# Attention and experts on one core: rank the experts three slots earlier, split the early weight pieces in halves, free the output scatters of one another, and run the 256-row group ahead of the 128-row one

## The chip, the cores and the metric

One core of one Trainium2 chip runs the whole program. The metric is the device time of one execution in microseconds (us), the median of several runs. Lower is better. PE is the matmul engine (TensorE), DVE VectorE, ACT ScalarE, POOL GpSimd, and SP SyncE, which here only issues DMAs.

## The reference

Attention over 8 batches of 8 heads, 576 positions of 64 numbers, with a mask by blocks of 64; its output, 4608 rows of 512 numbers, goes through a layer of eight experts, of which each row uses the one with the highest logit.

```python
scores = scale * np.matmul(q, k.transpose(0, 1, 3, 2))
scores = np.where(mask, scores, -1000000000.0)      # block_i >= block_j
attn = np.exp(scores - np.max(scores, axis=-1, keepdims=True))
attn = attn / (np.sum(attn, axis=-1, keepdims=True) + 1e-09)
x = np.matmul(attn, v).transpose(0, 2, 1, 3).reshape(B * S, H * D)
logits = x @ w_gate + modality_bias[modality_id]
e_idx = np.argmax(logits, axis=1)
gate_w = probs[np.arange(N), e_idx]
for e in range(E):
    mask = e_idx == e
    h = np.maximum(x[mask] @ w1[e], 0.0)
    out[mask] = gate_w[mask, None] * (h @ w2[e])
```

## The kernel before

The program has two halves. The first is attention in 32 **slots**, one for each pair of heads, and one more slot that drains (`LAST`). A slot runs the pieces of two pairs, interleaved by the table `ORDER`: of pair `slot` the scores (`S0`, `S1`, ... on PE), the row maxima (`M`, DVE), the exponentials (`E`, ACT), the transposes (`T`) and their copies (`C`); of pair `slot - 1` the product with the values (`V`), its way back to rows (`B`, `Z0`, `Z1`). Two pieces run ahead. `L` loads q and k of pair `slot + 2` (tile `raw`, a DMA on SP's queue), and `Q` scales q of pair `slot + 1` on POOL (`scale`, line 193, four instructions). The scores of the next slot can't start before that scaling is done. Engines take their instructions in the order in which the code writes them.

After every four slots a batch is complete. Its rows are stored to the tensor `xrows` in HBM, and `routing` finds each row's expert and its place in that expert's list. The places are written to `idlist` in HBM by five indirect scatters on POOL for each batch (line 401). `choose` ranks the experts after three batches: the largest is "a", the next "b", and a third one, "c", gets what is chosen later.

While attention still runs, the experts' work is begun at the points that `EARLY_STEPS` names. `chosen` and `stage` read the rank into a register and load pieces of expert a's weights to one of two `staging` tiles. `prep` splits a piece on POOL into a high part (a cast, line 596) and a low part (a subtraction, line 597), four of each for a piece. `ids` loads the head of expert a's list, and `fetch` gathers rows by an indirect DMA on POOL (line 698).

The second half is the experts in **groups** of rows, one after another: a 256-row group and a 512-row group of the early ("lead") list, three 512-row groups of a, four of b, then a 128-row group that ends b's list, then a 256-row group of c. For each group:

- `gather` (line 698) brings the rows by indirect DMAs on POOL, four for each 128 rows, into the tile `xg[1]`, which is part of `xr`;
- `turn_rows` (lines 717 to 721) turns them in four steps (two for 256 rows): a transpose on DVE into a `room` of two buffers, a cast to the high part on ACT, and a subtraction for the low part on DVE;
- `up` (line 730) multiplies with the first weights, eight blocks of 12 matmuls, and takes each block out by ACT and DVE (lines 733, 734); the 128-row group has `up_few` and `turn_few` instead;
- `down` (line 770) multiplies with the second weights, scales by the gate on ACT (line 774) into one of four tiles `yos`, and scatters 128 rows to the output by an indirect DMA on POOL (line 775).

For group n the code writes first the gathers of group n + 1, then the `up`s of n, `turn_rows` of n + 1, and the second part of `down` of n with its scatters. The first gather of a list also calls `spread` (lines 681 to 690), which on POOL makes row numbers, ids and gates out of the list. All output scatters write one tensor, so by the framework's rule each waits for the landing of the one before. `declare_no_dep` takes that wait away; the scatters to `idlist` use it already (line 403).

Of the kernel before, what the change touches and what calls it, by code (L numbers as in the profile page):

```python
# [16 lines left out]
ALU = mybir.AluOpType  # L17
# [29 lines left out]
WIDE = 4  # L47
# [28 lines left out]
)  # L76

EARLY_STEPS = {
    (20, "S0"): ("chosen", "stage", "stage"), (21, "S0"): ("ids",), (21, "T0"): ("prep",),
    **{(slot, "T0"): ("stage", "prep") for slot in range(22, 29)},  # L80
    **{(slot, "S0"): ("fetch",) for slot in (23, 24, 25, 26, 27, 29, 31)},
    (30, "S0"): ("fetch", "stage"), (30, "T0"): ("fetch",) * 2, (31, "T0"): ("fetch",) * 2,
}
LAST = (
    ("+turn0", 0), ("V", 1), ("O", 1), ("D", 1), ("+up0", 0), ("+fetch3", 0), ("B", 1), ("Z0", 1), ("Z1", 1), ("+steps1", 0), ("+up1", 0), ("+fetch3", 0),
# [470 lines left out]
class Experts:  # L556
    def __init__(self, ctx, tc, cst, scratch, btmp, edges, xrows, idlist, idf, w1, w2, out, sel, run, base8, pick, dot, banks, ys, placing, staging, extra, xrb, xg0, steps_left):
        self.__dict__.update(locals())
        self.nc = tc.nc
        self.turn, self.hturn = 0, 0  # L560
        self.er, self.w = {}, {}
        self.staged = []
        self.todo = [(k, name, c) for name in "abc" for k in range(2) for c in range(4)]
        self.sturn, self.sbank = 0, 0
        flat = xrb[0].rearrange("p s q d -> p (s q d)")
        self.spare = xrb[1].rearrange("p s q d -> p (s q d)")
        self.turned = 0
        self.xg = [t.rearrange("p (c w) -> p c w", w=PIECE) for t in (xg0, flat[:, 0:2048])]
        self.yos = [t[:, 512 * i : 512 * i + 512] for t in (scratch, xg0) for i in range(2)]
        self.pieces = xrows.rearrange("n (i w) -> (n i) w", w=PIECE)  # L570

        def cut(i, a, n=1024):
            return extra[:, i : i + n].rearrange("p (a f) -> p a f", a=a)

        self.w["a", 1] = [[cut(1024 * (4 * x + c), 2) for c in range(4)] for x in range(2)]
        self.xth = cut(1024 * 8, 4, 2048)
        self.xtl = self.xth[:, :, 256:512]
        self.hidden = extra[:, 1024 * 10 : 1024 * 14]
        self.w["a", 0] = [cut(1024 * 14 + 4096 * x, 4, 4096) for x in range(2)]
        self.parts = []  # L580
# [5 lines left out]
    def early(self, what):  # L586
        if what == "stage":
            self.stage()
        elif what == "chosen":
            assert not self.steps_left("c")  # L590
        elif what == "prep":
            st, k, name, c = self.staged[0]
            flat = [t.rearrange("p a f -> p (a f)") if len(t.shape) > 2 else t for t in (st, *self.target(k, name, c))]
            for i in range(4):
                s, h, l = (t[:, 256 * i : 256 * i + 256] for t in flat)
                self.nc.gpsimd.tensor_copy(h, s)
                self.nc.gpsimd.tensor_tensor(l, s, h, ALU.subtract)
            self.staged.pop(0)
        elif what == "ids":
            ids = self.load_ids(self.sel["ra"], 0, LEAD, "lead", self.scratch[:, 512:1024])  # L600
            self.plan = [(ids, 0, "a", EARLY * S), (ids, 2, "a", EARLY * S, WIDE)]
        elif what[0:5] == "fetch":
            for _ in range(int(what[5:] or 1)):
                self.fetch_next()
        elif what[0:4] == "turn":
            self.turn_rows(self.parts[int(what[4])])
        elif what[0:2] == "up":
            for m in range(2):
                self.up(self.parts[0], 2 * int(what[2]) + m)
        elif what == "place":  # L610
            if self.placing:
                g, c = self.placing.pop(0)
                g(c)
        elif what == "flush":
            self.flush()
# [93 lines left out]
    def turn_rows(self, s):  # L709
        nc, n = self.nc, 4 * s.parts  # L710
        room = self.spare if self.turned else self.scratch
        self.turned += 1
        step = 1 if s.parts == WIDE else 2
        for k in range(0, 4, step):
            at = 512 * (k // step % 2)
            x = room[:, at : at + 32 * n * step].rearrange("p (k c t) -> p k c t", k=step, t=32)
# [1 line left out]
            xv = x.rearrange("p k c t -> p k (c t)")  # L718
            h, l = (t[:, k : k + step, 0 : 32 * n] for t in (self.xth, self.xtl))
            nc.scalar.copy(h, xv)  # L720
            nc.vector.tensor_tensor(l, xv, h, ALU.subtract)

    def up(self, s, m):
        nc, n = self.nc, 128 * s.parts
# [37 lines left out]
    def down(self, s, i, ms=range(8)):  # L762
# [7 lines left out]
            nc.tensor.matmul(y, s.hs[m][x][:, ts], self.part(w, 1, m // 2)[:, m % 2, :], start=first, stop=last)  # L770
        if ms[-1] != 7:
            return
        yo = self.yos[i]
        nc.scalar.mul(yo, y, s.list.gate[:, s.t + i : s.t + i + 1])
        nc.gpsimd.indirect_dma_start(self.out, bass.IndirectOffsetOnAxis(ap=s.list.ids[:, s.t + i : s.t + i + 1], axis=0), yo, None, bounds_check=N - 1, oob_is_err=False)  # L775

    def next_segment(self, name):
        dve, start = self.nc.vector, self.sel["start"]
# [17 lines left out]
    def lists(self):  # L796
# [10 lines left out]
        self.more = self.trips(left)  # L807
        self.plan += [(idsa, WIDE * t, "a", N, WIDE) for t in range(3)]
        self.plan += [(idsb, WIDE * t, "b", N, WIDE) for t in range(4)]
        self.plan += [(idsb, 4 * WIDE, "b", N, 1), (idsc, 0, "a")]  # L810

    def run_all(self, steps):
        tc, ctx, plan = self.tc, self.ctx, self.plan
# [13 lines left out]
        for n in range(1, len(plan)):  # L827
# [6 lines left out]
            else:  # L834
                for m in range(8):
                    self.up(s, m)
                    if m == 3:
                        for _ in range(2):
                            if self.staged:
                                self.convert()  # L840
                        if s.parts == WIDE:
                            for i in range(WIDE):
                                self.down(s, i, range(4))
            if nxt is not None:
                self.turn_rows(nxt)
            for i in range(s.parts):
# [81 lines left out]
```

## Time and profile before

| what | value |
|---|---|
| three runs, median (lowest to highest) | 733.03 us (731.99 to 733.95) |
| the profiled execution, its own time | 734.32 us |
| its span, first to last instruction | 732.4 us |
| PE busy | 702.7 us (96%) |
| DVE, ACT, POOL busy | 381.2, 334.6, 343.2 us |
| mean granted TensorE clock | 0.985 of full speed |

Busy times are shares of the whole span. A matmul's end is modelled, so a busy PE may still run slower than it could. What a stretch loses is therefore read from its length beside that of a like stretch, and from the idle times in it. The clock column says which share of full speed was granted: 1.00 is 2.4 GHz, and a mean between 0.5 and 1.00 is a stretch that was partly at 1.2 GHz.

### The profile page before, as it was taken

Reading aid. Unit: us, or ns where it says so; the run is one execution under the profiler, and the core shown is the slowest. Engines: PE = TensorE matmul, PEld = TensorE weight load, DVE = VectorE, ACT = ScalarE, POOL = GpSimd, SP = SyncE. Lnnn points to the kernel's source line nnn. Section 1 sums busy time; section 2 is a strip of 40 time slices with the busy share of each in tenths; the row PEclk is TensorE's granted clock in tenths of the full one; section 3 lists DMA queues with packets and bytes.
Section 4 is the critical chain, followed back from the end, with each engine's and each line's share of the span. In section 5 each row is a group of like instructions: output and inputs, shape, how many; then the busy total and the mean of one; then the engine's idle time right before and its main releaser. Section 6 shows DMA issues by size and latency. Waiting matters only on the chain. (4 is left out here: it accounts for less than half of the span.)

```text
span 732.4 us, 17917 instructions
## 1 busy us (share of the span) xinstructions
PE 702.7 (96%) x6880; PEld 578.8 (79%) x6880; DVE 381.2 (52%) x1069; ACT 334.6 (46%) x983; POOL 343.2 (47%) x454
## 2 busy tenths in 40 slices
PE   8999999999999899999999999999999999999594
PEld 5888888788878787878888888886888888888483
DVE  5888898898989798642422323213242331321130
ACT  5888877778777777221321313213132241312020
POOL 2223343252589996567356172561725437131501
PEclk9999999999999999999999999999999999999978
DMA  6376445446667573414032130311413123010100
GB/s 211 121 236 207 137 153 151 138 136 193 182 184 206 167 220 93 100 43 104 26 108 64 44 110 24 118 50 43 111 33 123 35 70 99 34 43 28 48 15 20
DMA packets 38472, 77.41 MB, mean 106 GB/s; under 512 B 8574, under 2 KB 20746, under 8 KB 38384
## 3 DMA queue, kind: packets, MB, share of 16 engines
q1 hardware_dynamic: 29264, 57.02, 25.8%
q0 software_dynamic: 9120, 19.22, 8.5%
q8 instruction: 55, 0.90, 0.5%
q14 instruction: 33, 0.27, 0.1%
HBM read 54.84 MB, written 21.95 MB: 105 GB/s over the span
## 5 line engine op out<-in xcount | busy, mean ns | idle before, releaser
L231 ACT ACTIVATE pm<-bank,nm 128x512 f32<-128x512 f32 (+3 forms) x320 | 155.5, 501 | 64.9 <-DVE nm L218 64.1
L734 DVE SCALAR_TENSOR_TENSOR extra<-bank,extra 128x512 fp32r<-128x512 f32 (+1 forms) x80 | 50.9, 637 | 213.7 <-ACT extra L733 213.6
L733 ACT ACTIVATE extra<-bank 128x512 fp32r<-128x512 f32 (+1 forms) x80 | 44.4, 555 | 214.4 <-PE bank L730 214.4
L218 DVE TENSOR_REDUCE nm<-bank 128x1 f32<-128x512 f32 (+3 forms) x320 | 120.6, 445 | 7.7 <-PE bank L211 7.6
L730 PE MATMUL bank<-extra 128*128 128x512 f32 (+1 forms) x416 | 105.9, 356 | 9.7 <-ACT extra L720 9.6
L193 POOL TENSOR_SCALAR q<-raw 128x144 f32<-128x144 f32 x124 | 68.1, 583 | 67.8 <-DMA raw<-qk 45.5
L211 PE MATMUL bank<-raw,q 64*64 64x512 f32 (+7 forms) x1280 | 91.1, 416 | 4.0 <-POOL q L193 3.3
L238 PE MATMUL bank<-cf,pm 128*128 128x128 f32 (+1 forms) x736 | 90.2, 277 | 2.1 <-ACT pm L231 2.1
L730 PEld LDWEIGHTS bank<-extra 128*128 128x128 f32 x416 | 71.7, 195 | 21.4 <-ACT extra L720 11.1
L238 PEld LDWEIGHTS bank<-cf,pm 128*128 128x128 f32 (+1 forms) x736 | 78.4, 140 | 10.9 <-ACT pm L231 7.0
L211 PEld LDWEIGHTS bank<-raw,q 64*64 64x64 f32 x1280 | 56.4, 136 | 34.2 <-issue 22.1
L698 POOL DMA_INDIRECT xr<-xrows,row_b x68 | 70.4, 1035 | 21.0 <-issue 19.5
L401 POOL DMA_INDIRECT idlist<-idt,pi x40 | 40.8, 1020 | 74.5 <-DVE pi L400 40.8
L257 PE MATMUL b<-pt,v 64*64 64x64 f32 (+3 forms) x896 | 75.4, 267 | 0.2
L257 PE MATMUL o<-pt,v 64*64 64x64 f32 (+3 forms) x896 | 70.6, 262 | 0.8 <-DVE gl L297 0.8
L243 DVE COPY pt<-bank 128x512 f32<-128x512 f32 (+1 forms) x96 | 59.0, 642 | 17.3 <-PE bank L238 11.3
L231 ACT ACTIVATION_READ_ACCUMULATOR pm<-bank,nm 128x1 f32 x320 | 65.2, 204 | 0.0
L730 PE MATMUL bank<-xtl,extra 128*128 128x512 f32 (+1 forms) x160 | 60.5, 378 | 0.0
L720 ACT CAST extra<-xr 128x512 fp32r<-128x512 f32 (+1 forms) x36 | 21.9, 609 | 84.2 <-DVE xr L717 84.2
L698 POOL DMA_INDIRECT xr<-xrows,row_a x48 | 50.8, 1058 | 15.2 <-issue 14.6
L770 PE MATMUL bank<-extra 128*128 128x512 f32 x240 | 56.0, 389 | 0.0
L257 PEld LDWEIGHTS b<-pt,v 128*64 128x64 f32 (+1 forms) x896 | 53.3, 136 | 3.0 <-DVE pos L380 0.2
(182 smaller groups left out, 1172.5 us busy)
## 6 DMA issues: line engine op xcount, KB each, us to landing
raw<-qk SPq DMA_DIRECT2D x31, 576.0 KB, 4.0
v<-vr SPq DMA_DIRECT2D x32, 384.0 KB, 3.8
staging<-w SPq DMA_DIRECT2D x48, 128.0 KB, 3.5
staging<-w SPq DMA_DIRECT2D x12, 512.0 KB, 3.8
xrows<-xr SPq DMA_DIRECT2D x16, 256.0 KB, 4.4
xrows<-xr SPq DMA_DIRECT2D x32, 128.0 KB, 2.6
idlist<-btmp SPq DMA_DIRECT2D x8, 304.0 KB, 3.8
xr<-xrows,row_b POOLq DMA_INDIRECT x68, 2.6
```

Of the source, the lines that this page charges most:

```text
L193: pool.tensor_scalar(d.q[:, i : i + 144], d.raw[:, i : i + 144], SCALE, None, ALU.mult)
L211: pe.matmul(place(s, a, b)[64 * t : 64 * t + 64], d.q[hs, D * s : D * s + D], d.k[hs, a:b], start=True, stop=True)
L218: dve.tensor_reduce(d.nm[:, i : i + 1], place(s, a, b), AX.X, ALU.max, negate=True)
L231: act.activation(d.pm[:, o : o + b - a], place(s, a, b), AF.Exp, bias=d.nm[:, s : s + 1], scale=1.0, accum_out=total)
L238: pe.transpose(banks[g][0:m, 128 * i : 128 * i + 128], d.pm[:, o : o + m], idf)
L243: dve.tensor_copy(dst, src) if g in ON_DVE else act.copy(dst, src)
L257: pe.matmul(o.rearrange("p (n c) -> p n c", c=64), d.v[rows, h, block, :], x, start=start, stop=stop)
L698: self.nc.gpsimd.indirect_dma_start(s.xg[:, i, :], None, self.pieces[0 : 4 * s.nrows, :], bass.IndirectOffsetOnAxis(ap=row, axis=0), bound ...
L730: nc.tensor.matmul(hp, w[:, kc, ms], x[:, kc, 0:n], start=i == 0, stop=i == len(mm) - 1)
L733: nc.scalar.activation(hh, hp, AF.Relu)
L734: nc.vector.scalar_tensor_tensor(hl, hp, 0.0, hh, ALU.max, ALU.subtract)
L770: nc.tensor.matmul(y, s.hs[m][x][:, ts], self.part(w, 1, m // 2)[:, m % 2, :], start=first, stop=last)
```

## The change

1. `EARLY_STEPS`: the ranking is read and two weight pieces are staged in slot 17 in place of 20; the list's head is loaded in slot 20 in place of 21. A `prep` now does half a piece (two casts and two subtractions), and the 16 halves stand in slots 18 to 30 (two in 19, 21 and 22, else one) where eight whole pieces stood in slots 21 to 28. The next piece is staged right behind a piece's second half. The first gathers move by a slot or less.
2. `turn_rows`: a step's subtraction is written behind the next step's transpose.
3. `down`: a 256-row group writes its results to `yos` 2 and 3. Scatters of the lists a, b and c are declared free of one another.
4. `lists` and `run_all`: the 256-row group of c runs ahead of the 128-row group of b, and the lists of b and c are spread in groups 2 and 3, ahead of their first gathers.

```diff
+HALVES = {18: 1, 19: 2, 20: 1, 21: 2, 22: 2, **{slot: 1 for slot in range(23, 31)}}
 EARLY_STEPS = {
-    (20, "S0"): ("chosen", "stage", "stage"), (21, "S0"): ("ids",), (21, "T0"): ("prep",),
-    **{(slot, "T0"): ("stage", "prep") for slot in range(22, 29)},
-    **{(slot, "S0"): ("fetch",) for slot in (23, 24, 25, 26, 27, 29, 31)},
-    (30, "S0"): ("fetch", "stage"), (30, "T0"): ("fetch",) * 2, (31, "T0"): ("fetch",) * 2,
+    (17, "S0"): ("chosen", "stage", "stage"), (20, "S0"): ("ids",),
+    **{(slot, "T0"): ("prep",) * n for slot, n in HALVES.items()},
+    **{(slot, "S0"): ("fetch",) for slot in range(23, 32)},
+    (30, "V"): ("fetch",), (31, "V"): ("fetch",), (31, "T0"): ("fetch",),
 }
...
-            for i in range(4):
+            for i in range(2 * self.half, 2 * self.half + 2):
                 s, h, l = (t[:, 256 * i : 256 * i + 256] for t in flat)
                 self.nc.gpsimd.tensor_copy(h, s)
                 self.nc.gpsimd.tensor_tensor(l, s, h, ALU.subtract)
-            self.staged.pop(0)
+            self.half = 1 - self.half
+            if not self.half:
+                self.staged.pop(0)
+                self.stage()
...
-        step = 1 if s.parts == WIDE else 2
+        step, lows = 1 if s.parts == WIDE else 2, []
...
             nc.scalar.copy(h, xv)
-            nc.vector.tensor_tensor(l, xv, h, ALU.subtract)
+            lows.append((l, xv, h))
+            if len(lows) > 1:
+                nc.vector.tensor_tensor(*lows.pop(0), ALU.subtract)
+        nc.vector.tensor_tensor(*lows.pop(0), ALU.subtract)
...
-        yo = self.yos[i]
+        yo = self.yos[i + 2 if s.parts == 2 else i]
...
+        if s.list.name in "abc":
+            for other in self.outs:
+                self.tc.declare_no_dep(last.ins, other.ins, reason="each token stands once in these lists")
+            self.outs.append(last)
...
-        self.plan += [(idsb, 4 * WIDE, "b", N, 1), (idsc, 0, "a")]
+        self.plan += [(idsb, 4 * WIDE, "b", N, 1)]
+        self.plan.insert(-1, (idsc, 0, "a"))
...
+            if n in (2, 3):
+                self.spread(self.plan[5 if n == 2 else 9][0])
             if nxt is not None:
                 self.turn_rows(nxt)
```

How the instructions stand is shown at three places. First, POOL's queue between the scaling of pair 26 and that of pair 27, before: two scatters of places (`idlist`), one whole weight piece, a gather, and the scaling (`q`), on which the scores of slot 27 wait.

```order
L401 DMA idlist<-idt,pi_3844 38912x16
L596 CAST extra<-staging_80 128x256
L597 TENSOR_TENSOR extra<-staging_80,extra 128x256
L596 CAST extra<-staging_80 128x256
L597 TENSOR_TENSOR extra<-staging_80,extra 128x256
L596 CAST extra<-staging_80 128x256
L597 TENSOR_TENSOR extra<-staging_80,extra 128x256
L596 CAST extra<-staging_80 128x256
L597 TENSOR_TENSOR extra<-staging_80,extra 128x256
L401 DMA idlist<-idt,pi_3845 38912x16
L698 DMA xg_82<-xrows,row_lead 128x128
L193 TENSOR_SCALAR q_105<-raw_103 128x144 x4
```

The same place after the change:

```order
L402 DMA idlist<-idt,pi_3858 38912x16
L597 CAST extra<-staging_81 128x256
L598 TENSOR_TENSOR extra<-staging_81,extra 128x256
L597 CAST extra<-staging_81 128x256
L598 TENSOR_TENSOR extra<-staging_81,extra 128x256
L402 DMA idlist<-idt,pi_3859 38912x16
L702 DMA xg_82<-xrows,row_lead 128x128
L194 TENSOR_SCALAR q_105<-raw_103 128x144 x4
```

Half the piece has gone from this place; it stands in an earlier slot.

Second, POOL's queue at the end of the program, before, from the gathers of the 128-row group (`row_b`, four of them) on: `out` is the output, `ids_b` and `ids_c` the lists that the scatters go by, `row_c` and `both_c` what `spread` makes.

```order
L698 DMA xr_83<-xrows,row_b 128x128 x4
L775 DMA out<-scratch,ids_b 4608x512 x2
L775 DMA out<-xg_82,ids_b 4608x512 x2
L687 TENSOR_SCALAR row_c<-xr_84 32x8 x4
L689 COPY both_c<-xr_84 32x4 x4
L690 CAST ids_c<-both_c 128x2
L698 DMA xr_83<-xrows,row_c 128x128 x8
L775 DMA out<-scratch,ids_b 4608x512
L775 DMA out<-scratch,ids_c 4608x512 x2
```

And after:

```order
L702 DMA xr_83<-xrows,row_c 128x128 x8
L782 DMA out<-scratch,ids_b 4608x512 x2
L782 DMA out<-xg_82,ids_b 4608x512 x2
L702 DMA xr_83<-xrows,row_b 128x128 x4
L782 DMA out<-xg_82,ids_c 4608x512 x2
L782 DMA out<-scratch,ids_b 4608x512
```

The eight gathers of c have moved ahead of the four scatters of the last 512-row group of b, and the spreading of c's list has left this place. The four gathers of the 128-row group now stand behind those scatters.

Third, DVE's queue where the 512-row group of the early list is turned, before (`xtl` is the low part) and after:

```order
L717 STREAM_TRANSPOSE xr_84<-xr_83 128x512
L721 TENSOR_TENSOR xtl<-xr_84,extra 128x512
L717 STREAM_TRANSPOSE xr_84<-xr_83 128x512
L721 TENSOR_TENSOR xtl<-xr_84,extra 128x512
L717 STREAM_TRANSPOSE xr_84<-xr_83 128x512
L721 TENSOR_TENSOR xtl<-xr_84,extra 128x512
L717 STREAM_TRANSPOSE xr_84<-xr_83 128x512
L721 TENSOR_TENSOR xtl<-xr_84,extra 128x512
```

The queue after the change, at the same group:

```order
L721 STREAM_TRANSPOSE xr_84<-xr_83 128x512 x2
L727 TENSOR_TENSOR xtl<-xr_84,extra 128x512
L721 STREAM_TRANSPOSE xr_84<-xr_83 128x512
L727 TENSOR_TENSOR xtl<-xr_84,extra 128x512
L721 STREAM_TRANSPOSE xr_84<-xr_83 128x512
L727 TENSOR_TENSOR xtl<-xr_84,extra 128x512
L728 TENSOR_TENSOR xtl<-xr_84,extra 128x512
```

Each subtraction stands one transpose later.

## Rows read from the trace of the kernel before

**Rows 1.** Waits of PE: who for whom, us in total, times, longest.

```profile
PE bank L730 <- ACT extra L720: 11.1, 5, 8.6
PE bank L211 <- POOL q L193: 3.3, 2, 1.8
```

**Rows 2.** Stretches, one attention slot each (19, 21 to 27): length, engines busy, clock, DMA.

```profile
core 0: us, PE busy (x) PEld busy (x) DVE busy (x) ACT busy (x) POOL busy (x), PEclk, DMA share, GB/s
171.90:180.62 8.72, 8.72 (x172) 7.40 (x166) 7.80 (x26) 7.60 (x27) 3.63 (x8) 1.00 0.47 136
189.17:197.91 8.74, 8.74 (x172) 7.45 (x167) 8.03 (x24) 7.45 (x27) 5.65 (x10) 1.00 0.50 150
197.91:206.72 8.81, 8.81 (x170) 7.10 (x164) 8.30 (x30) 6.61 (x26) 8.11 (x14) 1.00 0.94 239
206.72:217.22 10.50, 9.00 (x173) 7.53 (x163) 9.05 (x30) 7.97 (x27) 9.07 (x21) 1.00 0.51 150
217.22:225.76 8.54, 8.54 (x153) 7.15 (x157) 7.17 (x23) 6.51 (x25) 7.94 (x15) 1.00 0.66 208
225.76:234.71 8.95, 8.95 (x174) 7.57 (x165) 7.77 (x24) 7.49 (x27) 8.17 (x13) 1.00 0.60 190
234.71:245.42 10.71, 8.90 (x158) 7.26 (x156) 9.59 (x35) 7.34 (x27) 9.69 (x15) 1.00 0.91 278
245.42:256.11 10.69, 10.56 (x157) 8.39 (x158) 6.84 (x21) 7.25 (x25) 9.73 (x16) 0.84 0.24 70
```

**Rows 3.** Timeline of POOL: start, us, instruction, idle time before it and its releaser.

```profile
194.77 1.03 POOL L401 DMA_INDIRECT idlist<-idt,pi  x1 [2.89 <-DVE pi L400]
...
235.93 0.41 POOL L596 CAST extra<-staging 128x256 fp32r<-128x256 f32 x1
...
240.76 1.02 POOL L401 DMA_INDIRECT idlist<-idt,pi  x1 [0.15 <-DVE pi L400]
242.09 1.04 POOL L698 DMA_INDIRECT xg<-xrows,row_lead  x1 [0.30 <-issue]
243.16 2.20 POOL L193 TENSOR_SCALAR q<-raw 128x144 f32<-128x144 f32 x4
```

**Rows 4.** Waits of SP's queue for POOL's weight splits: total, times, longest.

```profile
SPq L659 <- POOL extra L597: 3.8, 2, 2.6
```

**Rows 5.** Timeline of DVE at the starts of `turn_rows`: lead's 512 rows, b's first, c.

```profile
316.99 0.71 DVE L717 STREAM_TRANSPOSE xr<-xr 128x512 f32<-128x512 f32 x1 [5.59 <-DMA xr<-xrows,row_lead]
318.44 0.69 DVE L721 TENSOR_TENSOR xtl<-xr,extra 128x512 fp32r<-128x512 f32 x1 [0.74 <-ACT extra L720]
...
494.06 0.71 DVE L717 STREAM_TRANSPOSE xr<-xr 128x512 f32<-128x512 f32 x1 [6.36 <-DMA xr<-xrows,row_b]
...
695.26 0.71 DVE L717 STREAM_TRANSPOSE xr<-xr 128x512 f32<-128x512 f32 x1 [11.45 <-DMA xr<-xrows,row_c]
```

**Rows 6.** Stretches of the experts' half, with the columns of rows 2.

```profile
320.77:333.77 13.00, 12.00 (x50) 8.77 (x48) 7.49 (x24) 4.20 (x7) 7.06 (x14) 1.00 0.19 63
410.00:420.88 10.88, 10.88 (x50) 9.01 (x49) 2.08 (x3) 2.61 (x5) 2.76 (x3) 1.00 0.19 73
497.05:512.16 15.11, 13.57 (x49) 9.86 (x48) 5.39 (x8) 5.62 (x10) 2.97 (x3) 0.89 0.14 52
682.20:696.67 14.47, 5.88 (x27) 4.34 (x25) 1.97 (x4) 1.20 (x2) 8.39 (x10) 0.87 0.09 24
696.67:711.73 15.06, 15.01 (x96) 14.27 (x97) 4.96 (x10) 3.89 (x9) 1.01 (x1) 0.78 0.05 18
711.73:722.80 11.07, 11.07 (x50) 8.83 (x48) 0.42 (x1) 1.07 (x2) 0.99 (x1) 1.00 0.04 15
722.80:732.40 9.60, 0.00 (x1) 0.00 (x0) 0.00 (x0) 0.69 (x1) 0.97 (x1) 0.73 0.05 20
```

**Rows 7.** Timeline of POOL: scatters to the lists, an output scatter, the spreading of c.

```profile
318.27 0.97 POOL L401 DMA_INDIRECT idlist<-idt,pi  x1 [0.31 <-issue]
...
672.43 1.00 POOL L775 DMA_INDIRECT out<-scratch,ids_b  x1 [2.52 <-DMA out<-scratch,ids_b]
...
680.47 0.97 POOL L687 TENSOR_SCALAR row_c<-xr 32x8 int32<-32x8 f32 x4
```

More of the change, by code (lines that the diff above doesn't have):

```diff
@@ L561, in __init__ @@
         self.er, self.w = {}, {}
-        self.staged = []
+        self.staged, self.half, self.outs = [], 0, []
         self.todo = [(k, name, c) for name in "abc" for k in range(2) for c in range(4)]
@@ L772, in down @@
             return
-        yo = self.yos[i]
+        yo = self.yos[i + 2 if s.parts == 2 else i]
         nc.scalar.mul(yo, y, s.list.gate[:, s.t + i : s.t + i + 1])
-        nc.gpsimd.indirect_dma_start(self.out, bass.IndirectOffsetOnAxis(ap=s.list.ids[:, s.t + i : s.t + i + 1], axis=0), yo, None, bounds_check=N - 1, oob_is_err=False)
+        last = nc.gpsimd.indirect_dma_start(self.out, bass.IndirectOffsetOnAxis(ap=s.list.ids[:, s.t + i : s.t + i + 1], axis=0), yo, None, bounds_check=N - 1, oob_is_err=False)
+        if s.list.name in "abc":
+            for other in self.outs:
+                self.tc.declare_no_dep(last.ins, other.ins, reason="each token stands once in these lists")
+            self.outs.append(last)
     def next_segment(self, name):
```

## The prediction

> **What bounds the kernel now.** PE does, nearly everywhere; what can be won is the time in which it stands still or runs slowly behind a stand-still. I read the waits of PE first [rows 1]. Two releasers matter: the cast in `turn_rows` (11.1 us in five waits, one of them 8.6) and the scaling of q on POOL (3.3 us in two). Idle time alone says too little, so each place is measured as a stretch, from one landmark on PE to the next, against a like stretch without trouble.
>
> In the attention half the landmarks are the first score matmuls of the slots [rows 2]. Undisturbed slots take 8.72, 8.74 and 8.81 us (19, 21, 22); the length goes round with the slot's place in its batch, so slots 23 and 27 are held against 19, 25 against 21, and 26 against 22. Then slot 23 loses 10.50 - 8.72 = 1.8, slot 25 0.2, slot 26 1.9 and slot 27 2.0 us. The reader is to see the POOL column in those rows: 9.07, 9.69 and 9.73 us busy in slots of 10.5 to 10.7. Slot 27 has another cause than slot 26: PE is busy for 10.56 of 10.69 us, but at a mean clock of 0.84. It pays for the pause at the end of slot 26 by running partly at 1.2 GHz.
>
> In the experts' half four blocks of `up` take 10.88 us when nothing waits [rows 6]. Where lead's 512-row group begins, the same four took 13.00; where b's first group begins, 15.11. Ahead of c's group 14.47 us pass in which only one `down` has work, 11.07/2 = 5.5 us by the two `down`s of c. Then c's `up`s take 15.06 us at a clock of 0.78. DVE's timeline tells why [rows 5]: at b's first group and at c the first transpose waited for the gathered rows, 6.36 and 11.45 us. At lead's group it waited too, and there the steps themselves then run one after another: 1.45 us from a transpose to its subtraction, of which 0.74 is waiting for the cast.
>
> **The change part by part.** *Halved pieces.* On POOL a whole piece takes 240.76 - 0.15 - 235.93 = 4.7 us, a scatter 1.0 and a gap, the gather 1.04 + 0.30, the scaling 2.2 [rows 3]. With two scatters a slot's list is thus about 10.6 us long, and slot 26, which has exactly this list, is 10.71 long. Half a piece leaves 8.3 us, under the 8.7 to 8.8 of PE. Slots 23 to 30 have half a piece each, so POOL catches up by 2.3 us in slot 23 already, and the scalings for slots 25 to 28 come in time. Gain: 0.2 + 1.9 + 2.0 = 4.1 us, the clock's part in it. Bounds: nothing, if something else on POOL keeps the scalings late, and 4.1.
>
> Slot 23 keeps its loss. Slots 21 and 22 have whole pieces still, and slot 23 begins with the spreading of the early list: from the scatter at 194.77, which waits for DVE in any case, to the scaling for slot 24 POOL's queue reads the same before and after. So 1.8 us stay. What follows such a pause is not fixed: behind slot 23 (1.5 us of pause) the clock row shows 1.00 and a slot of 8.54 us; behind slot 26 (1.8 us) it shows 0.84 and 2.0 us lost [rows 2]. I go by the row of slot 23: no drop. The Trainium skill ("TensorE: Matmul & The Clock Gate", section "What's actually happening") says that the activity monitor is free-running and does not restart with the kernel, so by it the same pause may lower the clock in one program and not in another. By that rule the surviving pause could cost 2.0 us more, as in slot 27; it is a rival below.
>
> *Ranking in slot 17, the list's head in slot 20.* The eight staging DMAs leave SP's queue at slot 20 and stand at slot 17, ahead of a `raw` load. DVE writes the rank in slots 14 to 16, so nothing waits for it. POOL has room for the first halves: it is busy for only 3.63 of 8.72 us in slot 19. Cost: nothing; without that cover, a scaling late by as much as the load is.
>
> *Staging behind the second half.* This adds a wait on SP: the DMA into a staging tile waits for POOL's subtraction of the same slot, and the loads of v and `raw` are queued behind it. Such waits exist before too, 3.8 us in two, the longest 2.6 [rows 4], and they held no score matmul. A `raw` load is issued two slots ahead of its scores and scaled one slot ahead, which leaves about a slot of slack. Cost: nothing, at most one slot's worth of lateness for each of the eight pieces.
>
> *`turn_rows` pipelined.* The transpose of the next step now fills the 0.74 us gap. From the rows' durations (0.71, 0.74, 0.69) four steps come to about 5.5 us in place of 8.2. At lead's 512-row group the rows arrive when they did, and the last low part is ready some 2.7 us sooner; PE lost 13.00 - 10.88 = 2.1 us there and loses nothing then. In the first turn of 256 rows, within slot 32, one of two such gaps goes: 0 to 0.7, taken as 0.4, since PE has other work beside it. Elsewhere the turn is hidden behind `down`, and gains nothing.
>
> *Scatters independent, lists spread early.* An output scatter waits 2.52 us for the one ahead to land [rows 7]; three such waits for each 512-row group go, 7.6 us by which the gathers behind them start earlier. The spreading of b's list leaves the path too. At b's first group the rows are thus there 7.6 us or more earlier, and PE lost 15.11 - 10.88 = 4.2 there. All of it comes back, the clock's part (0.89) with it. Whether the declaration takes effect, no output scatter shows; the bounds are 0 and 2.52 us each. I take 2.52, because scatters to the lists, which are declared so already, follow each other at 0.31 us of idle time. In the other groups nothing waits on PE, and nothing is gained.
>
> *c ahead of the 128-row group.* c's eight gathers came behind the four scatters of b's last group and the spreading at 680.47 [rows 7], when only the 128-row group covered them. Now they stand ahead of those four scatters, a whole 512-row group earlier. So the pause of 14.47 - 5.5 = 8.9 us goes, and so does the low clock behind it: 15.06 x (1 - 0.78) = 3.3 us. The four gathers of the 128-row group now come behind the scatters: 4 x 1.34 = 5.4 us and a landing, while PE has all of c's work, 15.06 - 3.3 + 11.07 = 22.8 us. They are in time. The new place of the results (`yos` 2 and 3) keeps c's scatters off the buffers that the 128-row group writes; no engine waits for that. The tail, 9.60 us from the last matmul to the end [rows 6], hangs on one gate multiplication and one scatter as before, and stays.
>
> **The sum.** 4.1 + 0.4 + 2.1 + 4.2 + 8.9 + 3.3 = 23.0 us. The profiled execution took 734.32 us (span 732.4 and 1.9 around it), which gives 711.3. It lies 1.3 us above the runs' median of 733.03, so the forecast for a median is **710.0 us**.
>
> **The rivals.**
> - *The clock drops behind slot 23.* For it: slot 27. Against it: slot 24 in this trace. 710.0 + 2.0 = 712.0 us. Chance 0.10.
> - *POOL stays late in slots 25 to 27*, because the halves moved into slots 18 to 22 leave a backlog there, or because DVE's scatter indices come late. For it: slots 21 and 22 keep whole pieces. Against it: 2.3 us are freed in every slot from 23 to 28. The 4.1 us stay away: 714.1 us. Chance 0.10.
> - *The 128-row group starves in c's place.* For it: its gathers stand behind four scatters. Against it: 22.8 us of cover for some 9 us. If half of c's old pause came back, 4.5 us: 714.5 us. Chance 0.06.
> - *Scatters still wait for one another.* Then 7.6 us a group remain on POOL, but c's gathers are moved all the same, and b's first group has the early spreading and the shorter turn: 1 to 2 us worse, 711.5. Chance 0.04.
> - *The stall of slot 23 goes too*, if POOL reaches it with less behind it. Against it: the wait for DVE at 194.77 resets its queue. 710.0 - 1.8 = 708.2 us. Chance 0.08.
> - *Slower than before.* The new waits on SP delay the `raw` loads. To eat 23 us, each of the eight staging points must cost PE 2.9 us; that begins only where SP is held for more than a slot, 8.7 us, and the longest such wait now is 2.6. 735 us or more. Chance 0.03.
>
> **How the numbers follow.** My forecast, between 708.5 and 711.5, has 0.59. From 707.0 to 715.0 us all but the last rival lie inside, with a little room at both ends for slots 29 to 32, where the halves now stand beside DVE's routing; I leave some 0.15 outside for what I have not seen. A measurement of this kernel can tell about 0.3%, 2.2 us, from no change. Faster than 730.8 is everything but the last rival and a mixture of several: 0.95; the same 0.02, slower 0.03.
>
> **What would show it.** Slots 25 to 28 at 8.5 to 8.8 us, slot 23 near 10.5. Where lead's 512-row group and b's first begin, four blocks of `up` in 10.9 us. DVE's first transpose for c not waiting for `row_c`, no pause on PE ahead of c, and its `up`s in about 11.7 us at a clock of 1.00. Output scatters about 1.3 us apart where their results are ready. 9.6 us after the last matmul. I am wrong if POOL's scalings still end PE's waits behind slot 24, or if SP's waits for the weight splits grow to a slot's length and `raw` comes late.

## The result and the profile after

The changed kernel takes 712.38 us (median of four runs, 712.20 to 712.77), the kernel before 733.49 in the same comparison (731.99 to 734.36). The ratio is 0.9715, with a 95% interval of 0.9697 to 0.9733. The forecast of 710.0 is 2.4 us too low, and the range of 707 to 715 holds the time. The profiled execution of the changed kernel took 712.77 us with a span of 710.8, that of before 734.32 with 732.4. So the span lost 21.6 us, where the sum had 23.0. The time also lies outside the narrower band of 708.5 to 711.5 us, which the prediction thought the likeliest.

First some of the waits of PE after the change (line, releaser, us in total, times, longest), which answer to [rows 1].

```profile
PE bank L239 <- ACT pm L232: 2.0, 2, 1.5
PE bank L212 <- POOL q L194: 1.6, 1, 1.6
PE b L544 <- DVE long L165: 1.3, 1, 1.3
...
PE bank L763 <- DVE scratch L756: 0.3, 1, 0.3
PE b L258 <- DVE pos L381: 0.2, 1, 0.2
```

The cast in `turn_rows`, 11.1 us before, is no longer in the view. Of the two waits for POOL's scaling one is left, 1.6 us. The others belong to the attention half and (line 763) to the 128-row group.

The stretches of the attention slots 23 to 27, and in the last row the value matmuls of slot 31, answer to [rows 2] and have its columns.

```profile
207.09:217.66 10.57, 9.01 (x174) 7.54 (x164) 9.10 (x30) 7.98 (x27) 9.08 (x21) 1.00 0.52 169
217.66:226.20 8.54, 8.54 (x154) 7.15 (x158) 7.19 (x23) 6.52 (x25) 7.71 (x14) 1.00 0.32 110
226.20:235.01 8.81, 8.81 (x172) 7.43 (x166) 8.00 (x24) 7.15 (x27) 6.99 (x11) 1.00 0.83 266
235.01:243.83 8.82, 8.82 (x170) 7.11 (x163) 8.31 (x30) 6.76 (x26) 7.30 (x11) 1.00 0.64 174
243.83:252.55 8.72, 8.72 (x171) 7.40 (x166) 8.38 (x26) 7.53 (x27) 7.85 (x12) 1.00 0.57 195
282.55:288.74 6.19, 5.98 (x88) 4.96 (x79) 5.77 (x22) 5.72 (x23) 2.95 (x4) 1.00 0.39 101
```

Slots 25 to 27 have lengths of undisturbed slots, and POOL is busy for 7.0 to 7.9 us in them, not 8.2 to 9.7. Slot 23 keeps its 10.57 us. Slot 24 behind it runs at a clock of 1.00. The last row was 5.78 us long before (from the starts of its matmuls), so 0.41 us have come in there, for which the prediction has no term.

The stretches of the experts' half answer to [rows 6]: four blocks of `up` of lead's 512-row group and of b's first group, the `up`s of c, its two `down`s, the two `up_few` of the 128-row group, its `down`, and what is left to the end (that last row still holds the end of the `down`, 0.51 us of PE).

```profile
317.36:328.24 10.88, 10.88 (x49) 9.01 (x48) 6.09 (x22) 3.58 (x6) 6.96 (x13) 1.00 0.24 76
491.44:502.32 10.88, 10.88 (x49) 9.01 (x48) 2.08 (x3) 2.49 (x4) 7.58 (x8) 1.00 0.27 83
665.52:677.03 11.51, 11.51 (x97) 11.50 (x96) 2.98 (x7) 3.38 (x8) 5.03 (x5) 1.00 0.21 68
677.03:687.94 10.91, 10.91 (x50) 9.02 (x49) 1.86 (x5) 1.81 (x4) 1.01 (x1) 1.00 0.05 17
687.94:693.39 5.45, 5.45 (x26) 4.46 (x25) 0.00 (x0) 1.29 (x2) 0.99 (x1) 1.00 0.08 31
694.74:700.20 5.46, 5.46 (x26) 4.24 (x25) 1.34 (x2) 0.59 (x1) 0.00 (x0) 1.00 0.00 0
700.20:710.80 10.60, 0.51 (x3) 0.09 (x1) 0.00 (x0) 0.69 (x1) 0.97 (x1) 0.66 0.08 27
```

None of these stretches but the last has idle time on PE, and in all but the last the clock is 1.00. From the start of c's `up`s to the end 45.28 us pass; the same work (128-row group and c) took 57.03 before, from 675.36 to 732.39.

POOL's timeline shows the output scatters (`out`) of the last group of a, then those of the last 512-row group of b with the first gather of the 128-row group (start, us, idle time before it and its releaser). They answer to the scatter in [rows 7].

```profile
444.16 1.06 POOL L782 DMA_INDIRECT out<-scratch,ids_a  x1 [13.66 <-ACT scratch L781]
445.52 0.99 POOL L782 DMA_INDIRECT out<-scratch,ids_a  x1 [0.30 <-issue]
446.82 0.98 POOL L782 DMA_INDIRECT out<-xg,ids_a  x1 [0.30 <-issue]
449.09 0.97 POOL L782 DMA_INDIRECT out<-xg,ids_a  x1 [1.28 <-ACT xg L781]
...
658.90 1.01 POOL L782 DMA_INDIRECT out<-scratch,ids_b  x1 [24.27 <-ACT scratch L781]
661.25 0.99 POOL L782 DMA_INDIRECT out<-scratch,ids_b  x1 [1.34 <-ACT scratch L781]
663.97 0.97 POOL L782 DMA_INDIRECT out<-xg,ids_b  x1 [1.73 <-ACT xg L781]
666.69 0.98 POOL L782 DMA_INDIRECT out<-xg,ids_b  x1 [1.75 <-ACT xg L781]
667.97 1.04 POOL L702 DMA_INDIRECT xr<-xrows,row_b  x1 [0.30 <-issue]
```

The declaration took effect: where results are ready, the scatters follow at 1.3 to 1.4 us. But the last one, and all of the later group, wait for the gate multiplication (line 781), which in that later group gives a result each 2.4 to 2.7 us.

DVE's timeline, three places: the last scatter index (`pi`) and the copy behind it, the first transposes for b's first group, and those for c. The second and third answer to [rows 5].

```profile
280.31 0.50 DVE L401 TENSOR_TENSOR pi<-pp,cf 128x1 int32<-128x1 f32 x1
280.74 0.54 DVE L244 COPY pt<-bank 128x384 f32<-128x384 f32 x1
...
482.00 1.29 DVE L721 STREAM_TRANSPOSE xr<-xr 128x512 f32<-128x512 f32 x2
...
656.08 1.30 DVE L721 STREAM_TRANSPOSE xr<-xr 128x512 f32<-128x512 f32 x2
```

The first transposes for b and c show no idle time ahead of them now; before they waited 6.36 and 11.45 us for rows. The first of these lines took 0.50 us for 128 numbers. Beside it stands, on POOL, a subtraction of a weight half that the change has put into slot 30:

```profile
280.07 0.73 POOL L598 TENSOR_TENSOR extra<-staging,extra 128x256 fp32r<-128x256 f32 x1
```

It ends at 280.80, and the DVE instruction at 280.81.

Last, the waits of SP's queue for POOL's weight splits, which answer to [rows 4]:

```profile
SPq L663 <- POOL extra L598: 18.8, 4, 6.8
SPq L660 <- POOL extra L598: 10.0, 2, 8.7
```

Before, such waits came to 4.7 us in three, the longest 2.6. Now they are 28.8 us in six, and the longest is 8.7 us, a slot's length.

### The profile page after: what moved, and what is told of

Read it like the earlier page. It is cut to its first block, busy times and chain, and to the rows that moved or that the text cites. A ratio compares the mean times of both kernels' runs of the same rounds, so it can differ in the third digit from the quotient of the medians.

```text
span 710.8 us, 17930 instructions
## 1 busy us (share of the span) xinstructions
PE 693.8 (98%) x6880; PEld 574.2 (81%) x6880; DVE 380.8 (54%) x1069; ACT 336.5 (47%) x983; POOL 344.9 (49%) x454
## 4 chain that ended last, share of the span: by engine, by line
PE 87%; issue 5%; DVE 3%; ACT 2%; POOL 2%; POOLq 0%; DVEq 0%; ACTq 0%
PE bank L737 27%; PE bank L777 13%; PE bank L212 10%; PE bank L239 10%; PE o L777 7%; PE b L777 6%; PE o L258 5%; PE b L258 5%; PE o L278 2%; ACT pm L232 2%; DVE nm L219 1%; PE b L544 1%; PE b L278 0%; POOL out L782 0%; DVE pt L244 0%
## 5 line engine op out<-in xcount | busy, mean ns | idle before, releaser
L737 PE MATMUL bank<-extra 128*128 128x512 f32 (+1 forms) x416 | 102.8, 349 | 0.0
L239 PEld LDWEIGHTS bank<-cf,pm 128*128 128x128 f32 (+1 forms) x736 | 78.3, 140 | 11.1 <-ACT pm L232 6.6
L737 PEld LDWEIGHTS bank<-extra 128*128 128x128 f32 x416 | 69.8, 189 | 10.3 <-issue 0.2
L737 PE MATMUL bank<-xtl,extra 128*128 128x512 f32 (+1 forms) x160 | 58.8, 368 | 0.0
L258 PEld LDWEIGHTS o<-pt,v 128*64 128x64 f32 (+1 forms) x896 | 50.3, 135 | 5.5 <-DVE gl L298 0.9
```

What stands on the lines that cost most here:

```text
L239: pe.transpose(banks[g][0:m, 128 * i : 128 * i + 128], d.pm[:, o : o + m], idf)
L258: pe.matmul(o.rearrange("p (n c) -> p n c", c=64), d.v[rows, h, block, :], x, start=start, stop=stop)
L737: nc.tensor.matmul(hp, w[:, kc, ms], x[:, kc, 0:n], start=i == 0, stop=i == len(mm) - 1)
```

## The experiments

The theory is the prediction's, with terms that can each be undone alone. What it left open is which part earns the gain at b's first group and at c: free scatters, early spreading, the pipelined turn, or the order of the groups. The rivals are that one part is enough, so that the others earn nothing, and that a part earns only together with another.

**Whole pieces again** (`e1_whole`), the steps of before, with the rest of the change kept:

```diff
-HALVES = {18: 1, 19: 2, 20: 1, 21: 2, 22: 2, **{slot: 1 for slot in range(23, 31)}}
 EARLY_STEPS = {
-    (17, "S0"): ("chosen", "stage", "stage"), (20, "S0"): ("ids",),
-    **{(slot, "T0"): ("prep",) * n for slot, n in HALVES.items()},
+    (20, "S0"): ("chosen", "stage", "stage"), (21, "S0"): ("ids",), (21, "T0"): ("prep", "prep"),
+    **{(slot, "T0"): ("stage", "prep", "prep") for slot in range(22, 29)},
...
                 self.staged.pop(0)
-                self.stage()
```

> Undoes the halving, the ranking in slot 17 and the moved first gathers alone: the whole weight pieces stand in slots 21 to 28 again, all else is as after the change. My theory: POOL's list in slots 25 and 26 is longer than a slot again, so slots 25 to 27 lose what they lost before, 4.0 us, and the 0.4 us that slot 31 loses after the change and the 0.2 of slot 18 go; together about 3.4 us slower than the changed kernel, near 715.8 us, with the mean clock of slot 27 near 0.84. Rival: the scalings are late for another reason (the ranking's place), and the pieces' size matters little; then under 1 us slower.

Measured: 715.61 us (715.51 to 715.70), 0.9766 of before [0.9745, 0.9787]. That is 3.2 more than the changed kernel. Its slots 25 to 27:

```profile
225.35:234.34 8.99, 8.99 (x174) 7.58 (x165) 7.80 (x24) 7.54 (x27) 8.20 (x13) 1.00 0.55 171
234.34:245.07 10.73, 8.91 (x157) 7.27 (x155) 9.65 (x35) 7.32 (x27) 9.72 (x15) 1.00 0.91 272
245.07:255.79 10.72, 8.87 (x157) 7.47 (x157) 8.04 (x24) 7.04 (x25) 9.76 (x16) 1.00 0.29 79
```

The losses are back, 4.1 us in three slots, and POOL is busy there for 8.2, 9.7 and 9.8 us again. The run also puts the ranking, the list's head and the first gathers back, so by itself it can't tell these from the halves; POOL's busy time, which whole pieces lengthen, speaks for the halves. Slot 31's value matmuls take 5.79 us again, which gives 0.4 back. The third row corrects the prediction: slot 27 is as long as before, but here at a clock of 1.00 and with PE idle for 1.85 us. POOL's list, busy for 9.76 us of it, sets the length: PE waits 1.85 us for POOL's scaling at its end. The lower clock of slot 27 before cost nothing on top of that.

**The 128-row group ahead of c again** (`e2_few_first`):

```diff
-        self.plan.insert(-1, (idsc, 0, "a"))
+        self.plan += [(idsc, 0, "a")]
...
-                self.spread(self.plan[5 if n == 2 else 9][0])
+                self.spread(self.plan[5 if n == 2 else 10][0])
```

> Puts the 128-row group ahead of the 256-row group of c again, and keeps all else of the change. My theory: c's gathers stand behind the last four scatters again, but these are 2.7 us apart now and the spreading is gone, so the rows come some 4 to 5 us earlier than before the change; a pause of 4 to 5 us is left ahead of c, and the clock falls behind it: 6 to 8 us slower than the changed kernel, 718 to 720 us. Rival one: the order is all, and the whole 11.8 us come back (724). Rival two: the free scatters and the early spreading are enough, and at most 1 us comes back.

Measured: 716.12 us (715.90 to 717.19), 0.9772 [0.9750, 0.9793]; 3.7 more than the changed kernel, about half of what was expected. The `down` ahead of c with the pause, and c's `up`s:

```profile
672.11:680.99 8.88, 5.87 (x28) 4.33 (x26) 2.54 (x5) 1.26 (x3) 4.54 (x5) 1.00 0.10 28
680.99:694.58 13.59, 13.37 (x96) 13.16 (x97) 4.24 (x9) 3.82 (x9) 1.01 (x1) 0.87 0.05 20
```

The pause is 3.4 us by the prediction's measure (8.88 - 5.5), not 8.9, and the `up`s behind it run at a mean clock of 0.87. So with the other parts in place this pause is shorter even without the new order; that it is the scatters and the spreading, and not the turn, `f3_end_as_before` shows below.

**Scatters wait for one another again** (`e3_dep`):

```diff
-        if s.list.name in "abc":
-            for other in self.outs:
-                self.tc.declare_no_dep(last.ins, other.ins, reason="each token stands once in these lists")
-            self.outs.append(last)
```

> Lets each output scatter wait for the one before again, and keeps all else. The prediction put b's first group, 4.2 us, to the free scatters. The theory after the trace: the early spreading and the shorter turn cover that place by themselves, so nothing comes back: within 0.5 us of the changed kernel, 712.4 us, with the scatters 3.5 us apart and no pause on PE. Rival, the prediction's: 2 to 4 us slower, with a pause where b's first group begins.

Measured: 711.86 us (711.00 to 712.35), 0.9714 [0.9691, 0.9736]. Nothing comes back. POOL's timeline at the last group of a shows that the waits are there:

```profile
443.37 1.06 POOL L782 DMA_INDIRECT out<-scratch,ids_a  x1 [7.16 <-ACT scratch L781]
446.92 0.99 POOL L782 DMA_INDIRECT out<-scratch,ids_a  x1 [2.49 <-issue]
450.40 0.97 POOL L782 DMA_INDIRECT out<-xg,ids_a  x1 [2.49 <-DMA out<-scratch,ids_a]
453.90 0.97 POOL L782 DMA_INDIRECT out<-xg,ids_a  x1 [2.54 <-ACT extra L740]
```

The fourth scatter starts 10.5 us behind the first, 4.9 in the changed kernel. Against the first scatter, the gathers for b's first group come 5.6 us later for that, and still early enough. With the rest of the change in place the declaration earns nothing that this run can tell.

**The turn serial again** (`e4_serial`):

```diff
-            if len(lows) > 1:
-                nc.vector.tensor_tensor(*lows.pop(0), ALU.subtract)
-        nc.vector.tensor_tensor(*lows.pop(0), ALU.subtract)
+            nc.vector.tensor_tensor(*lows.pop(0), ALU.subtract)
```

> Writes each subtraction of the turn right behind its cast again, as before the change, and keeps all else. Theory: lead's 512-row group loses its 2.1 us again, the first turn 0.3, and b's first group nothing, since the rows come early: 2.4 us slower than the changed kernel, 714.8 us. Rival: the rows for lead's group come early enough by themselves, and nothing is lost (712.4); or b's first group needs the short turn too (2.4 + 2 to 4 us, 717 to 719).

Measured: 714.85 us (714.58 to 715.36), 0.9756 [0.9734, 0.9777], as expected. Lead's 512-row group has its loss again, and no other group:

```profile
317.68:330.70 13.02, 12.03 (x49) 8.77 (x48) 7.49 (x24) 4.20 (x7) 7.06 (x14) 1.00 0.19 63
```

The first turn is back at 3.34 us from 3.06. b's first group keeps its 10.88.

**A second comparison, on another chip.** Every kernel, the one before among them (769.24 us), took about 5% longer there, with pauses on PE in the attention and the experts' half. For some of them the profile shows no releaser; others end with an ACT or DVE instruction that itself started late. What causes them is open, so these four runs don't compare in us with the rest. (A ratio is estimated from the executions, and lies up to 0.3% from the quotient of the two medians here.) Scatters waiting and lists spread late (`e5_dep_late`), with the edit of `e3_dep` and this one:

```diff
-            if n in (2, 3):
-                self.spread(self.plan[5 if n == 2 else 9][0])
```

> Lets each output scatter wait for the one before, and spreads the lists of b and c at their first gathers again; the pipelined turn and the order of the last groups stay. Theory: at b's first group the rows come as late as before the change, but the pipelined turn needs 1.3 us a step in place of 2.0 and so keeps ahead of PE, which loses at most 0.5 us: 712 to 713 us, b's first four blocks of the up product in 10.9 to 11.4 us. Rival: the late rows cost what they cost before, 4.2 us (716.6), and either of the free scatters and the early spreading is needed.

Measured: 745.38 us (743.07 to 754.54), 0.9664 of before [0.9631, 0.9698]. That and the serial turn (`e6_all_three`):

> As the run before, and the subtractions of the turn stand right behind their casts again: of the changes in the experts' half only the order of the last groups is left. Theory: b's first group loses its 4.2 us again, lead's 512-row group 2.1, the first turn 0.3: 6.6 us slower than the changed kernel, 719.0 us. Rival: b's first group does not lose them even so, since the program reaches it differently now; then 2.4 us slower, 714.8.

Measured: 754.24 us (750.34 to 756.21), 0.9786 [0.9753, 0.9819]. The third part undone costs about 1.2% here; where, the pauses hide. In both runs b's first four blocks take 10.88 us, but behind pauses of 1.5 and 4.9 us in the group ahead, so neither run decides between its theory and its rival.

More halves early, so that slots 21 and 22 have half a piece each (`e7_early`):

```diff
-HALVES = {18: 1, 19: 2, 20: 1, 21: 2, 22: 2, **{slot: 1 for slot in range(23, 31)}}
+HALVES = {18: 2, 19: 2, 20: 2, 21: 1, 22: 1, **{slot: 1 for slot in range(23, 31)}}
```

> The changed kernel with the halves earlier: two in slots 18, 19 and 20, one in 21 to 30. Theory: the 1.8 us that slot 23 still loses come from POOL's list in slots 21 to 23 (two halves each in 21 and 22, then the spreading of the early list); with 2.3 us less in slots 21 and 22 the scaling for slot 24 comes in time: slot 23 at 8.7 us, 1.8 us faster than the changed kernel, 710.6 us. Slot 31 keeps its 0.4. Rival: the wait for DVE's scatter index resets the queue late in slot 21, and the spreading alone makes slot 23 late: slot 23 at 9.5 or more.

Measured: 739.12 us, 0.9614 [0.9587, 0.9641]. Slot 23 takes 8.72 us, against 10.66 and 10.67 in the two kernels above on the same chip. And the same with slot 30 left free, whose half goes to slot 21 (`e8_early_clear30`):

```diff
-HALVES = {18: 1, 19: 2, 20: 1, 21: 2, 22: 2, **{slot: 1 for slot in range(23, 31)}}
+HALVES = {18: 2, 19: 2, 20: 2, 21: 2, 22: 1, **{slot: 1 for slot in range(23, 30)}}
```

> The halves two each in slots 18 to 21 and one in 22 to 29, none in slot 30. Theory: as the run before, and the product with the values in slot 31 takes 5.8 us again in place of 6.2, because the scatter index on DVE no longer stands beside a subtraction of POOL: 2.2 us faster than the changed kernel, 710.2 us. Rival: slot 31's 0.4 has another cause and stays (710.6); or two halves in slot 21 keep slot 23 late (712).

Measured: 741.07 us, 0.9616 [0.9583, 0.9649]. Slot 23 takes 8.68 us here too; between the two nothing can be told.

**Third comparison**, on a chip with the usual times (before: 733.03 us). All three parts undone, as in `e6_all_three` (`f1_all_three`):

> The kernel of the run with all three parts undone (scatters wait for one another, lists spread at their first gathers, subtraction right behind its cast), again, since every kernel on that chip, the one before too, took 36 us longer and engines paused for reasons that no wait shows. Theory as there: b's first group loses 4.2 us again, lead's 512-row group 2.1, the first turn 0.3: 6.6 us slower than the changed kernel, 719.0 us. Rival: b's first group loses nothing, 714.8.

Measured: 716.73 us (715.96 to 717.70), 0.9778 [0.9756, 0.9801], between theory and rival. Four blocks of `up` at lead's 512-row group and at b's first, second and fourth:

```profile
316.52:329.39 12.87, 11.99 (x49) 8.77 (x48) 7.38 (x24) 4.20 (x7) 6.99 (x14) 1.00 0.19 64
492.59:505.25 12.66, 11.88 (x50) 8.78 (x49) 4.77 (x8) 5.25 (x9) 2.34 (x3) 1.00 0.12 42
537.88:549.49 11.61, 11.45 (x49) 8.86 (x48) 4.08 (x6) 4.94 (x9) 2.94 (x3) 1.00 0.12 45
625.65:636.85 11.20, 11.20 (x49) 8.86 (x48) 4.00 (x6) 4.63 (x8) 2.65 (x3) 1.00 0.12 47
```

b's first group loses 1.8 us again, and two later ones 0.7 and 0.3, which lost nothing before (10.88 us each). The clock stayed at 1.00 at b's first group, where it was 0.89 before [rows 6]. So a loss at b's groups came back where all three parts were undone, but not at its size of 4.2. One difference can be named: in the kernel before, the first transpose of the group ahead waited 3.65 us for its rows, here 1.76, and its gate multiplications, scatters and gathers follow from it. Why those rows landed later is open.

Free scatters alone, with the two others undone (`f2_late_serial`):

> Lists spread at their first gathers and the subtraction right behind its cast, but the scatters free of one another: of the three parts, free scatters alone. The prediction said that they alone recover b's first group. Theory: they do (7.6 us earlier against a loss of 4.2), so that any one of the three is enough there: lead's group 2.1 and the first turn 0.3 lost, b's first group in 10.9 us, 714.8 us. Rival: the gathers start no earlier, since the results' buffers or the gate multiplications hold them: 2 to 4 us more, 717 to 719.

Measured: 714.22 us (713.94 to 714.32), 0.9743 [0.9723, 0.9763], near the theory's 714.8. b's first group:

```profile
493.02:503.90 10.88, 10.88 (x49) 9.01 (x48) 2.08 (x3) 2.49 (x4) 8.35 (x9) 1.00 0.34 121
```

**The end as before** (`f3_end_as_before`): the 128-row group ahead of c, scatters that wait, lists spread late; only the turn stays pipelined.

> The 128-row group ahead of c, scatters that wait for one another and lists spread at their first gathers: the program's end is as before the change, with the pipelined turn alone. Theory: the pause ahead of c is back at 8 to 9 us and the low clock behind it, so that with the run that undid the order alone (3.7 us) it shows what the free scatters and the early spreading were worth there, 7 us: about 11 us slower than the changed kernel, 723 us; b's first group loses nothing. Rival: the pipelined turn makes up for part of the pause, and it is 719 or less.

Measured: 721.74 us (721.09 to 722.36), 0.9847 [0.9826, 0.9869]; 9.4 more than the changed kernel. b's first group, the `down` and pause ahead of c, and c's `up`s:

```profile
490.02:500.90 10.88, 10.88 (x49) 9.01 (x48) 2.08 (x3) 2.49 (x4) 5.00 (x6) 1.00 0.21 79
670.96:684.71 13.75, 5.85 (x28) 4.33 (x26) 2.55 (x5) 1.26 (x3) 8.06 (x8) 0.82 0.09 25
684.71:698.85 14.14, 14.14 (x96) 13.92 (x97) 4.24 (x9) 3.82 (x9) 1.01 (x1) 0.81 0.05 19
```

The first row says that the pipelined turn alone is enough at b's first group. The other two say that the pause at c is back nearly whole, 13.75 us for 14.47 before, with the low clock behind it. Against `e2_few_first` c's gathers stand 4.9 us later (the last one starts 16.5 us behind the start of `up_few`, there 11.6): three scatters that wait 2.5 us in place of 1.7 for each other, and 2.7 us of spreading.

**More halves early and slot 30 free**, as in `e8_early_clear30`, on this chip (`f4_early_clear30`):

> The halves two each in slots 18 to 21 and one in 22 to 29, none in slot 30, again. On the slow chip slot 23 took 8.7 us in place of 10.7. Theory: slot 23 at 8.7 us and the product with the values in slot 31 in 5.8 us: 2.2 us faster than the changed kernel, 710.2 us. Rival: slot 31 keeps its 0.4 us (710.6).

Measured: 709.26 us (708.99 to 710.22), 0.9679 [0.9658, 0.9701], faster than both kernels and 3.1 us faster than the changed one, where 2.2 were expected. Slots 23 and 24, and the value matmuls of slot 31:

```profile
206.14:214.87 8.73, 8.73 (x171) 7.41 (x166) 8.32 (x27) 7.53 (x27) 7.31 (x18) 1.00 0.32 101
214.87:223.43 8.56, 8.56 (x170) 7.14 (x165) 8.19 (x28) 6.80 (x25) 7.11 (x12) 1.00 0.65 232
279.70:285.49 5.79, 5.79 (x88) 4.90 (x79) 5.37 (x21) 5.61 (x23) 2.51 (x4) 1.00 0.16 44
```

The stall of slot 23 is gone (1.8 us), and so is the 0.4 in slot 31. Little of the rest can be the edit's: between the two profiled executions 0.9 us lie in slots 0, 14 and 18, 0.1 in slot 25 and 0.4 behind the last gate multiplication. DVE's timeline has the index at 0.10 us, with nothing on POOL beside it:

```profile
277.46 0.10 DVE L401 TENSOR_TENSOR pi<-pp,cf 128x1 int32<-128x1 f32 x1
```

## Why the prediction was right, and where it was off

**Slots 25 to 27: right in size.** 30.35 us before, 26.35 after, 4.0 won for 4.1. `e1_whole` takes them back. One reason was wrong: the loss in slot 27 was read as the price of the clock, and it is POOL's list, by `e1_whole`. So the price of 2.0 us that the first rival put on a clock drop behind slot 23 had no row behind it. No drop came there, so the measured time is near that rival's 712.0 for other reasons, below. The Trainium skill ("TensorE: Matmul & The Clock Gate", section "What's actually happening") says that the activity monitor runs freely and doesn't start anew with a kernel; by that, like pauses may end differently. The traces agree: behind like pauses at the end of slot 26 slot 27 ran at 0.84 before and at 1.00 in `e1_whole`.

**Slot 23: right.** It kept 10.57 us. The argument that POOL's queue reads the same there holds for this change; half a piece less in slot 22 alone ends the stall, by `f4_early_clear30` (two halves in slot 21, one in 22).

**The pipelined turn: right.** 2.1 us at lead's group and 0.3 for 0.4 in the first turn; `e4_serial` takes 2.5 back. The four steps at lead's group took 5.6 us (from 313.49 to 319.08) in place of 8.2, as forecast.

**b's first group: right in size, the reason too narrow.** The 4.2 us were won, and 0.1 at the group ahead. But they were put down to scatters and spreading, with the gathers 7.6 us earlier. The gathers gain only 5.6 us by free scatters, since the fourth result isn't ready earlier, and they are not needed: free scatters alone are enough (`f2_late_serial`), the pipelined turn alone is enough (`f3_end_as_before`). Whether early spreading alone would be enough wasn't tried. By the order of the code, which no run tests link by link, the parts act on one ring of waits: the turn holds DVE and ACT, ACT's casts stand ahead of the gate multiplications, these release the scatters, the scatters stand ahead of the next gathers, and the gathers feed the next turn.

**c: right.** Predicted were 8.9 + 3.3 = 12.2. The end took 57.03 us before and takes 45.28 now, 11.75 less; 0.44 of the difference to 12.2 is the time from the start of the last gate multiplication to the end, 9.99 us in this execution and 9.55 before. In the ten traces from chips with the usual times it lies between 9.55 and 10.09, without order by kernel, so I don't count it as a cost of the change. The order of the groups alone is worth 3.7 us (`e2_few_first`), free scatters and early spreading without it 5.6 (721.74 - 716.12), both 9.4. Single executions stray by about a us from that: in the profiled ones the end takes 45.28, 50.08 and 55.41 us, which makes it 4.8, 5.3 and 10.1. From the start of `up_few` to the end `f3_end_as_before` takes 55.4 us, 1.6 less than before; that may be the turn's, which is all that is left of the change there, but it wasn't tried by itself.

**What the sum lacks.** The terms measured are 4.0 + 0.3 + 2.1 + 4.2 + 0.1 + 11.75 = 22.45 us. Against them 0.4 were lost in slot 31: the half piece in slot 30 collides with the scatter index on DVE. The seven traces with that half, from chips with the usual times, have 6.18 or 6.19 us there, and `e1_whole` and `f4_early_clear30`, which don't have it, 5.79. The prediction left room for "slots 29 to 32, where the halves now stand beside DVE's routing", and no term. Another 0.5 us were lost in the attention half of this execution, nearly all in slots 0, 14, 18 and 23. Slots 0, 14 and 18 differ as much or more from one execution to another: in the ten traces slot 0 takes 7.50 to 8.50 us, slot 14 9.23 to 9.49 and slot 18 8.81 to 9.00. 22.45 - 0.4 - 0.5 is 21.6, the difference of the spans. Last, the prediction took 1.3 us off for the profiled execution of before lying above the median; that of after lies only 0.4 above its own. So of the 2.4 us by which the forecast was too low, 1.5 are the sum's and 0.9 are this correction's.

No run undoes all of the experts' half at once. The 2.4 us at b's first group that `f1_all_three` doesn't bring back, and the 1.6 us at c, are gone in the trace after the change, but no experiment took them back.

**The other rivals.** POOL didn't stay late, the 128-row group doesn't starve (`up_few` starts without a wait and has none inside), and no score matmul waited for a `raw` load. But SP's waits for the splits did grow to a slot's length, the first half of the prediction's last sign of being wrong: 8.7 us at the longest, where the prediction knew of 2.6. That wait is for the half in slot 30, and every `raw` load had gone out before it (the last at 263.90, the wait from 272.07 to 280.81). Behind the next longest, 6.8 us, the `raw` load went out at 211.22, about 6 us ahead of its slot of scaling (217.66). So the loads' slack covered these waits, as the prediction argued, and the cost of nothing held. "Scatters still wait" was priced at 1 to 2 us; `e3_dep` shows nothing.

## What to carry to other kernels

Where several parts of a change relieve one ring of waits, undo them together as well as alone: undone alone, the free scatters looked worthless here, and at b's first group they were enough by themselves. A wait that goes gains no more than the next one leaves: the scatters were set free by 2.5 us each, but the results came 2.7 us apart. Where an engine's list is longer than the slot, it sets the slot's length at whatever clock, and the cure here was to move half a piece to a slot in which that engine had room.

## What the runs showed of the hardware

A DVE instruction on 128 numbers took 0.50 us in place of 0.10 beside a POOL subtraction and ended with it (280.81 and 280.80). The Trainium skill ("SBUF — State Buffer", section "Who interferes with whom") says that a DVE instruction with two SBUF inputs contends with a GpSimd instruction that reads SBUF, and that the port pair which they share is an exclusive lock. The rows agree: `pi` has two inputs, started behind the subtraction's start at 280.07, and took 0.10 where POOL did nothing. In the same trace the index took 0.49 and 0.52 us twice more, each time beside such a subtraction and ending within 0.02 us of it (225.75 and 225.74, 234.34 and 234.32). In slot 31 the delay reached PE: the copy behind it starts 1.17 us behind the slot's first score matmul (280.74 and 279.57), in `f4_early_clear30` 0.76, the stretch of the value matmuls took 0.40 longer, and the wait of PE for DVE's `pos` (line 381, 0.2 us) is in this trace and in neither `f4_early_clear30`'s nor `e1_whole`'s.
